# Two bytes instead of four for half words on the wire of a kernel's own clock

## The chip, the cores and the metric

One core of a Trainium2 chip. The metric is the device time of one execution in microseconds, from the first to the last instruction with what lies around them. TensorE is called PE in the profile, VectorE DVE, ScalarE ACT, GpSimd POOL, and SyncE, whose queue issues nearly all transfers, SP.

## The reference

Two blocks work on the same input `x` of 2048 tokens by 576 channels, and a gate mixes them. Cut to what matters:

```
g = sigmoid((x * gate_w).sum(-1))
# A: a long convolution; K is made from 128 complex exponentials per channel (the "taps")
K = einsum("dn,dnl,dn->dl", C, exp(dt * A * l), dt * B).real
a = irfft(rfft(u, 2L) * rfft(K, 2L))[:L] + u * Dskip
# B: product keys: 32 heads, two halves of 64 keys each, top 2 of both halves, 2 of the 4 pairs
q = x @ w_q;  s1 = q1 @ k1.T;  s2 = q2 @ k2.T
top_e, g2 = best two of the four sums and their softmax
act = gelu(x . u[top_e]);  b = sum(g2 * act * v[top_e])
return g * a + (1 - g) * b
```

## The kernel before, in words

The kernel computes dense what the reference gathers. There are two large families of products of half words (fp16, split in a high and a low part), each of 128 groups of 14 matmuls of 128 by 512: the scores `s` (tokens against keys, the query weights folded into the keys by small matmuls `wb`, after which DVE takes the 8 largest and their places) and the activations `a` (tokens against the 4096 rows of `u`), which are scaled into `go` and stored to `g_d` in DRAM.

Beside them run three stages of the convolution:

- The generation of the taps. Pairs of channel groups give matmuls `kb`; ACT and DVE split the result in half words `ko`, and 18 stores write it to `k_d`. In the same stretch a first transform of the input runs (`u`, with tables `tu`; results go to `su_d`).
- The first transform of the taps (`freq`, then `k_stage1`). Four loads, one for each quarter `j`, bring the taps back from `k_d` into the tile `ksb`, and two loads bring the tables `tk0` and `tk16`. Then come 32 steps `k1_0` to `k1_31` of 4 matmuls each, whose results are copied to `k1o` and stored to `sk_d`. All 128 of these matmuls read `ksb`; the first sixteen steps read `tk0`.
- The products in the frequency domain: 36 groups `pr`, `pi`, `pv`, with results stored to `z_d`.

When the scores and activations end, the kernel hands over to the last stage. For each of 16 blocks of 128 tokens, `prep` builds one-hot matrices on DVE (`A`, `Be`, `Bg`), spreads the gates with matmuls `S`, multiplies them into the activations `gl`, and splits the product into half words `wh`. Then 192 matmuls `o` multiply with the rows of `v`, which `v_work` has split into eight chunks `vhl0` to `vhl7`. A chunk costs two copies or scalings for each of four parts on ACT and four differences on DVE (some on POOL). The inverse transform `y` of the convolution is added to each block. The first blocks are 0, 15, 1 and 14.

Nobody writes the order of the instructions by hand. The source runs the whole program once on a clock of its own: every engine call adds a cost (`act_cost`, `dve_cost`, `mm`), every stage is a generator that yields until its inputs are ready by that clock, and the order in which the calls are made is the order in which the instructions stand in each engine's queue. On the chip the engines then wait for one another through semaphores; the source's clock has no part in that. So a cost that is changed moves instructions, and changes no instruction itself.

For transfers the function `dma` (L199) keeps two numbers: `queue`, with 0.45 for each issue, and `wire`, which grows by the bytes of the transfer at 3.4e5 bytes per microsecond. A tile counts as loaded 2.2 after `wire`. Two places read this: every generator that waits for a loaded tile, and the loop in `freq` that paces the loads of the taps:

```
for j in range(4):
    while wire[0] > clock[0] + 2:
        yield 0.3
    dma(ksb[:, j]..., k_d[:, 32 * j:32 * j + 32]...)
```

L133 is the one line through which all ACT, DVE and POOL instructions are recorded, L213 that of all matmuls, and L204 that of all transfers.

Of the kernel before, what the change touches and what calls it, by code (L numbers as in the profile page):

```python
# [13 lines left out]
F16 = mybir.dt.float16  # L14
BF16 = mybir.dt.bfloat16
# [122 lines left out]
def body(ctx: ExitStack, tc: tile.TileContext, xT, au, par, logdt, dskip, gatew, wq, kT, uT, vv,  # L138
# [11 lines left out]
    wire = [0.0]  # L150
# [5 lines left out]
    def key(x):  # L156
        n = x.tensor.name
        return (n, x.offset) if n in columns else n

    def size(x):  # L160
        n = 1
        for d in x.shape[1:]:
            n *= d
        return n
# [34 lines left out]
    def dma(o, i, q=None):  # L199
        t = max(clock[0], rdy.get(key(i), 0.0), queue[0])  # L200
        queue[0] = t + 0.45
        wire[0] = max(wire[0], t) + 4 * o.shape[0] * size(o) / 3.4e5
        rdy[key(o)] = max(rdy.get(key(o), 0.0), wire[0] + 2.2)
        (q or DQ).dma_start(o, i)  # L204

# [95 lines left out]
    def row(x, name, pool):  # L301
        t = pool.tile([128, D], F32, name=name)
        dma(t, bass.AP(tensor=x.tensor, offset=x.offset, ap=[[0, 128], [1, D]]))
        return t
# [7 lines left out]
    def au_load(a, t):  # L312
        for d, o in au_rows(au, t, a):
            dma(o, d)
# [108 lines left out]
    def x_load(tb):  # L423
        a = slot([4, 512], F32, f"xs{tb}")
        r = pl.tile([128, 512], F32, tag="xr", name=f"xr{tb}", bufs=2)
        c = slice(512 * tb, 512 * tb + 512)
        dma(a, xT[0:512, c].rearrange("(k p) n -> p k n", p=128))
        dma(r[0:64], xT[512:576, c])
        dma(r[64:128], xT[512:576, c])
        return a, r  # L430
# [1132 lines left out]
    while groups or acts:  # L1563
# [5 lines left out]
        if groups and bank_free() and lag < (6.0 if not a_ok else 2.0 if not turn_s else 5.0 if kdone[0] < NCK else 8.0):  # L1569
            c, t = groups[0]  # L1570
# [113 lines left out]
```

## Time and profile before

| | |
|---|---|
| median of 3 runs | 1466.44 us (1465.94 to 1466.64) |
| the profiled execution's own time | 1466.58 us |
| its span, first to last instruction | 1464.7 us |
| PE busy | 1431.2 us, 98% of the span |
| DVE busy | 1248.5 us, 85% |
| ACT busy | 790.6 us, 54% |
| POOL busy | 532.0 us, 36% |
| mean granted TensorE clock | 0.995 |
| read from and written to DRAM | 147.51 and 71.30 MB |

Busy shares are of the whole span. Matmuls overlap in the pipeline, so PE can be busy while one matmul waits for nothing but its turn; what counts for the end is where PE stands idle with work left. Times in the views are microseconds from the start of the span. A row of a timeline gives start, duration, engine, line, operation, output tile, input tiles, form and count, and in brackets the idle time before it and what ended that.

### The profile page before, as it was taken

What the parts mean: (1) busy time and instruction counts of PE and PEld (TensorE: products, weight loads), DVE (VectorE), ACT (ScalarE), POOL (GpSimd) and SP (SyncE); (2) the same over time, 40 slices, a digit from 0 to 9 for tenths busy, and PEclk for the clock granted to TensorE, in tenths of its full rate; (3) what the DMA queues carried; (4) which work ended last, traced back from release to release, by engine and by line L of the source; (5) the groups of instructions that cost most, each with busy time, mean ns of one, the idle gap of its engine ahead of it and who ended that gap; (6) DMA issues with size and microseconds to landing.
All of it is one profiled execution on the core that took longest, in us unless ns stands there. A gap on an engine that the chain in (4) does not pass through costs nothing.

```text
span 1464.7 us, 36789 instructions
## 1 busy us (share of the span) xinstructions
PE 1431.2 (98%) x14025; PEld 858.4 (59%) x14028; DVE 1248.5 (85%) x4589; ACT 790.6 (54%) x1315; POOL 532.0 (36%) x511
## 2 busy tenths in 40 slices
PE   5999999999999999999999999998999999999999
PEld 2445454554544544555555444455787787788787
DVE  6989989989999699959899898579998998898860
ACT  5647767698697787434656544576424224223310
POOL 0443545556745645201246799622100110110100
PEclk8999999999999999999999999999999999999999
DMA  9235433372434534384768666677533432442400
GB/s 319 81 93 162 128 94 118 111 213 89 147 104 133 160 107 135 109 263 138 254 211 290 232 200 206 221 239 221 157 111 116 133 125 85 138 147 68 156 10 17
DMA packets 139185, 221.21 MB, mean 151 GB/s; under 512 B 11648, under 2 KB 82688, under 8 KB 132608
## 3 DMA queue, kind: packets, MB, share of 16 engines
q1 hardware_dynamic: 138912, 218.78, 46.5%
q8 instruction: 110, 1.80, 0.5%
q14 instruction: 67, 0.55, 0.1%
q10 hardware_dynamic: 96, 0.07, 0.0%
HBM read 147.51 MB, written 71.30 MB: 149 GB/s over the span
## 4 chain that ended last, share of the span: by engine, by line
PE 84%; DVE 10%; DMA 3%; ACT 1%; issue 1%; SPq 1%; POOL 1%; DVEq 0%; ACTq 0%; POOLq 0%
PE o L213 24%; PE a L213 23%; PE s L213 22%; PE S L213 4%; PE wb L213 2%; PE kb L213 2%; DVE i L133 2%; PE pr L213 2%; DVE m L133 1%; PE u L213 1%; PE y L213 1%; PE kP L213 1%; DVE e L133 1%; PE pv L213 1%; DVE uh L133 1%
## 5 line engine op out<-in xcount | busy, mean ns | idle before, releaser
L213 PE MATMUL o<-vhl,wh 128*128 128x288 f16 x3072 | 387.0, 286 | 0.0
L213 PE MATMUL s<-whl,xb 128*128 128x512 f16 x1536 | 369.5, 382 | 5.0 <-DVE whl L133 4.2
L213 PE MATMUL a<-xb,uhl 128*128 128x512 f16 x1536 | 361.1, 379 | 0.4 <-DVE ko L133 0.4
L213 PEld LDWEIGHTS <-wh 128*128 128x128 f16 x3072 | 296.0, 98 | 76.3 <-issue 3.7
L213 PEld LDWEIGHTS <-xb 128*128 128x128 f16 x1792 | 171.8, 98 | 213.1 <-issue 27.1
L213 PEld LDWEIGHTS <-uhl 128*128 128x128 f16 x1536 | 148.2, 98 | 175.7 <-issue 2.8
L133 DVE FIND_INDEX8 i<-m,s 128x8 uint32<-128x64 f32 x1024 | 206.5, 222 | 0.0
L133 ACT ACTIVATE wh<-gl,s_wg 128x1024 f16<-128x1024 f32 x64 | 68.9, 1137 | 200.3 <-DVE gl L133 200.3
L133 DVE MAX8 m<-s 128x8 f32<-128x64 f32 x1024 | 146.4, 215 | 28.1 <-PE s L213 27.8
L133 POOL TENSOR_TENSOR CS<-CS,ex 128x512 f32<-128x512 f32 x72 | 100.2, 1423 | 139.0 <-DVE ex L133 120.0
L133 POOL TENSOR_TENSOR ya<-ya,db 128x576 f32<-128x576 f32 x16 | 32.0, 2012 | 305.2 <-DMA ya<-in_au_dram 143.6
L133 ACT ACTIVATE go<-a,i_a 128x512 f32<-128x512 f32 x95 | 64.2, 686 | 82.5 <-PE a L213 54.7
L133 POOL TENSOR_TENSOR e<-aN,rt 128x512 f32<-128x512 f32 x72 | 87.5, 1234 | 50.9 <-PE kb L213 47.6
L133 DVE SCALAR_TENSOR_TENSOR wh<-gl,s_wg,wh 128x1024 f16<-128x1024 f32 x64 | 92.4, 1474 | 11.3 <-ACT wh L133 11.3
L133 DVE TENSOR_TENSOR gl<-S,gl 128x256 f32<-128x256 f32 x256 | 90.0, 415 | 7.3 <-PE S L213 7.3
L133 DVE TENSOR_TENSOR Bg<-Be,vals 128x1024 f16<-128x1024 f16 x128 | 90.6, 749 | 2.2
L133 ACT ACTIVATE gl<-gl 128x1024 f32<-128x1024 f32 x64 | 63.5, 1045 | 34.8 <-DMA gl<-g_d 34.8
L133 DVE TENSOR_TENSOR A<-iota_a,vals 128x2048 f16<-128x2048 f16 x64 | 80.5, 1258 | 0.0
L213 PE MATMUL S<-Bg,A 128*128 128x64 f16 x2048 | 73.0, 193 | 5.1 <-DVE Bg L133 4.2
L213 PEld LDWEIGHTS <-A 128*128 128x128 f16 x2048 | 70.6, 97 | 11.2 <-DVE Bg L133 4.1
L213 PE MATMUL s<-wrem,xb 128*128 128x512 f16 x256 | 76.2, 379 | 0.0
L213 PE MATMUL a<-xb,wrem 128*128 128x512 f16 x256 | 76.2, 379 | 0.0
(203 smaller groups left out, 2205.7 us busy)
## 6 DMA issues: line engine op xcount, KB each, us to landing
g_d<-go SPq DMA_DIRECT2D x128, 256.0 KB, 2.7
gl<-g_d SPq DMA_DIRECT2D x32, 1024.0 KB, 5.4
wq<-in_wq_dram SPq DMA_DIRECT2D x16, 1152.0 KB, 6.3
us<-in_au_dram SPq DMA_DIRECT2D x64, 144.0 KB, 3.0
su_d<-us SPq DMA_DIRECT2D x32, 288.0 KB, 2.6
sk_d<-k1o SPq DMA_DIRECT2D x32, 288.0 KB, 2.8
vn<-in_vv_dram SPq DMA_DIRECT2D x32, 288.0 KB, 3.7
ui<-su_d SPq DMA_DIRECT2D x16, 576.0 KB, 4.0
```

Of the source, the lines that this page charges most:

```text
L133: return f(*a, **k)
L213: T.matmul(o, l, r, start=start, stop=stop)
```

## The change

One factor in `dma`. Until now each element of a transfer counted four bytes on the wire; now an element counts two where the destination is fp16 or bf16.

```
     def dma(o, i, q=None):
         t = max(clock[0], rdy.get(key(i), 0.0), queue[0])
         queue[0] = t + 0.45
-        wire[0] = max(wire[0], t) + 4 * o.shape[0] * size(o) / 3.4e5
+        wire[0] = max(wire[0], t) + (2 if o.dtype in (F16, BF16) else 4) * o.shape[0] * size(o) / 3.4e5
         rdy[key(o)] = max(rdy.get(key(o), 0.0), wire[0] + 2.2)
         (q or DQ).dma_start(o, i)
```

By the shapes, four kinds of transfer are counted anew, on the source's clock: a load of `ksb` (128 x 18 x 256 half words) from 6.94 to 3.47, a table `tk` (128 x 4096) from 6.17 to 3.08, a store of `ko` (128 x 1024) from 1.54 to 0.77, and a table `tu` (128 x 256) from 0.39 to 0.19. All other transfers are of 4-byte elements. The number and the forms of the instructions stay; their order changes on every engine from the generation of the taps on, up to about the fifth token block, and is the same again after that.

The first place is SP's queue at the loads of the taps. `go6_1_1` and its like are activations on their way to `g_d`, `wq5_1` is the second half of the query weights of chunk 5. Before:

```order
L204 DMA k_d_68<-ko_7597 128x1024
L204 DMA ksb_7659<-k_d_68 128x18x256
L204 DMA wq4_1_7753<-in_wq_dram 128x2304
L204 DMA g_d_65<-go6_1_0_7783 128x4x128
L204 DMA ksb_7659<-k_d_68 128x18x256
L204 DMA g_d_65<-go6_1_1_7804 128x4x128
L204 DMA g_d_65<-go6_1_2_7823 128x4x128
L204 DMA g_d_65<-go6_1_3_7844 128x4x128
L204 DMA ksb_7659<-k_d_68 128x18x256
L204 DMA wq5_0_7905<-in_wq_dram 128x2304
```

Here follow two more stores to `g_d`, the fourth load of `ksb`, and the two tables. Now:

```order
L204 DMA k_d_68<-ko_7824 128x1024
L204 DMA ksb_7855<-k_d_68 128x18x256
L204 DMA g_d_65<-go6_1_1_7865 128x4x128
L204 DMA ksb_7855<-k_d_68 128x18x256
L204 DMA wq5_1_7982<-in_wq_dram 128x2304
L204 DMA ksb_7855<-k_d_68 128x18x256 x2
L204 DMA tk0_8070<-in_tk_dram 128x4096
L204 DMA tk16_8072<-in_tk_dram 128x4096
```

Eight transfers stood between the first and the fourth load of `ksb`, apart from the loads of `ksb` themselves; now two stand there. On PE, the last matmuls of the generation (`kb34`) and the first step `k1_0` had 17 groups of `s` and `a` and three halves of the fold `wb` between them; now they have 120 matmuls of such groups (eight and a half) and two halves of `wb`. `k1_0` itself stands inside the same group as before, `s4_7`, but with 102 groups of `a` ahead of it instead of 106.

The second place is DVE's queue at the handover, between the one-hot matrices of the second part of block 15 and the first product with its gates (`gl15_0<-S15_0_0`). Before:

```order
L133 TENSOR_TENSOR Bg15_1_13111<-Be15_1_13109,vals_80 128x1024 x2
L133 SCALAR_TENSOR_TENSOR wh0_1_13094<-gl0_0_12547,s_wg_92,wh0_0_13093 128x1024
L133 SCALAR_TENSOR_TENSOR vhl4_12478<-vhl5_12686,sci_76,vhl4_12478 128x576
L133 SCALAR_TENSOR_TENSOR wh0_1_13094<-gl0_0_12547,s_wg_92,wh0_0_13093 128x1024
L133 SCALAR_TENSOR_TENSOR wh0_1_13094<-gl0_1_12548,s_wg_92,wh0_0_13093 128x1024
L133 SCALAR_TENSOR_TENSOR vhl5_12686<-vhl6_12687,sci_76,vhl5_12686 128x576
L133 TENSOR_SCALAR go7_2_0_13218<-a7_2_0_13149,i_a_91 128x512
L133 TENSOR_TENSOR gl15_0_13096<-S15_0_0_13179,gl15_0_13096 128x32x8
```

Now:

```order
L133 TENSOR_TENSOR Bg15_1_13173<-Be15_1_13171,vals_80 128x1024 x2
L133 SCALAR_TENSOR_TENSOR wh0_1_13102<-gl0_1_12722,s_wg_92,wh0_0_13101 128x1024
L133 SCALAR_TENSOR_TENSOR vhl7_12691<-vs_12937,sci_76,vhl7_12691 128x576
L133 SCALAR_TENSOR_TENSOR wh0_1_13102<-gl0_1_12722,s_wg_92,wh0_0_13101 128x1024
L133 TENSOR_SCALAR go7_2_2_13284<-a7_2_2_13218,i_a_91 128x512
L133 TENSOR_TENSOR gl15_0_13158<-S15_0_0_13250,gl15_0_13158 128x32x8
```

At this point the splitting of `v` stood at chunks 4 and 5 and now stands at the last, 7. From the last gates of block 0 (`S0_3`) on, DVE had seven differences of `vhl` still ahead of it and now has three; the other four stand ahead of `S0_3`, after the last scores.

More of the change, by code (lines that the diff above doesn't have):

```diff
@@ L201, in dma @@
         queue[0] = t + 0.45
-        wire[0] = max(wire[0], t) + 4 * o.shape[0] * size(o) / 3.4e5
+        wire[0] = max(wire[0], t) + (2 if o.dtype in (F16, BF16) else 4) * o.shape[0] * size(o) / 3.4e5
         rdy[key(o)] = max(rdy.get(key(o), 0.0), wire[0] + 2.2)
```

## The prediction

> **What bounds the kernel now.** I read the page first: the span, the busy shares, the slices and the chain of work that ended last.
>
> ```profile
> span 1464.7 us, 36789 instructions
> PE 1431.2 (98%) x14025; PEld 858.4 (59%) x14028; DVE 1248.5 (85%) x4589; ACT 790.6 (54%) x1315; POOL 532.0 (36%) x511
> ...
> PE   5999999999999999999999999998999999999999
> DVE  6989989989999699959899898579998998898860
> ...
> PEclk8999999999999999999999999999999999999999
> ...
> PE 84%; DVE 10%; DMA 3%; ACT 1%; issue 1%; SPq 1%; POOL 1%; DVEq 0%; ACTq 0%; POOLq 0%
> ```
>
> PE is busy 1431.2 of 1464.7 us, so all that an order can win or lose at once is the 33.5 us in which PE stands idle, and whatever new idle time it makes. The change removes no instruction and alters none, so the sum is a sum of waits. The next view is therefore the list of what PE waited for (total, times, longest, in us).
>
> ```profile
> PE x L213 <- ACT xb L133: 4.5, 1, 4.5
> PE S L213 <- DVE Bg L133: 4.2, 6, 2.3
> PE s L213 <- DVE whl L133: 4.2, 1, 4.2
> PE sq L213 <- ACT uhl L133: 4.0, 1, 4.0
> PE kn L213 <- ACT vals L133: 3.1, 1, 3.1
> PE pi L213 <- DVE m L133: 1.7, 1, 1.7
> PE k L213 <- ACT k1o L133: 1.4, 1, 1.4
> PE y L213 <- DMA tf<-in_tf_dram: 1.0, 1, 1.0
> PE kb L213 <- issue: 1.0, 1, 1.0
> ...
> PE S L213 <- DVE ya L133: 0.7, 1, 0.7
> ...
> PE k L213 <- DVE i L133: 0.6, 1, 0.6
> ```
>
> The waits for `xb`, `whl`, `uhl` and `vals` (15.8 us together) belong to the start, where the order is the same in both kernels; they stay. What is open to the change is short: the two waits of the taps' transform (`k`, 2.0 us), the one of the products (`pi`, 1.7), and the handover (`S` and `y`, up to 5.9). None of them is a wait for the taps' loads: at the place that the change is about, PE does not wait today.
>
> **The loads of the taps, the price.** Now the change, first where it acts: the four loads of `ksb`. Their time and PE's work around them before:
>
> ```profile
> 606.43 0.29 PE L213 MATMUL kb<-e,CS 128*32 128x64 f32 x8
> ...
> 638.68 2.75 PE L213 MATMUL s<-whl,xb 128*128 128x512 f16 x12
> ...
> 641.70 2.75 PE L213 MATMUL s<-whl,xb 128*128 128x512 f16 x12
> ...
> 652.20 2.32 PE L213 MATMUL wb<-kt,wq 128*64 128x64 f32 x72
> 654.45 1.47 PE L213 MATMUL s<-whl,xb 128*128 128x512 f16 x6
> 662.88 0.65 PE L213 MATMUL k<-ksb,tk 128*128 128x288 f16 x4
> ```
>
> From the last `kb` (606.43) to `k1_0` (662.88) lie 56.5 us, and `k1_0` shows no wait: 56.5 us of cover were enough for loads that went out over 28 us. The new order leaves 120 matmuls of groups `s` and `a` and two halves of `wb`. A group of 14 takes 3.02 us (638.68 to 641.70), so 120 take 120/14 x 3.02 = 25.9; a half of `wb` takes 2.25 (652.20 to 654.45), two 4.5; with the 0.29 of `kb` itself, **PE reaches `k1_0` 30.7 us after the start of the last `kb`.**
>
> What must have landed by then is `ksb` whole and `tk0`. The rows for it (in the windows: start and end, length, then busy PE, PEld, DVE, ACT, POOL, the granted clock, the DMA share and GB/s):
>
> ```profile
> 612.57 0.77 SPq L204 DMA_DIRECT2D ksb<-k_d  x1
> ...
> 640.16 0.68 SPq L204 DMA_DIRECT2D ksb<-k_d  x1
> ```
>
> ```profile
> DMA to landing us min/median/max: 6.7/6.8/6.9
> ```
>
> ```profile
> 614.60:617.60 3.00, 3.00 (x65) 2.11 (x64) 3.00 (x25) 0.52 (x1) 0.00 (x0) 1.00 0.95 274
> 619.40:621.40 2.00, 2.00 (x11) 0.90 (x10) 1.99 (x7) 0.70 (x3) 0.00 (x0) 1.00 1.03 438
> 648.40:651.40 3.00, 3.00 (x15) 1.36 (x14) 2.72 (x26) 0.00 (x0) 0.00 (x0) 1.00 1.02 428
> ```
>
> The first window holds a `ksb` load alone: 274 GB/s at a DMA share of 0.95, so the engines are full, and the short pieces of this gather, not the queue, set its pace. By its shape a load is 1.18 MB, at 274 GB/s 4.3 us; of the landing's 6.8 that leaves 2.5 of latency. The second window holds a load of `wq` (1.18 MB, at 438 GB/s 2.7 us), the third a table `tk` (1.05 MB, at 428 GB/s 2.45 us). In the new queue stand the four loads, one `g_d` store (0.26 MB, 1.0 us at the slow rate), `wq5_1` and `tk0`. The first load goes out 612.57 - 606.43 = 6.1 us after `kb`, since its stores to `k_d` come first, and I keep that. Then 6.1 + 2.5 + 4 x 4.3 + 1.0 + 2.7 + 2.45 = **32.0 us**, which is 1.3 behind PE. `wq5_1` has to wait on SP for PE to finish with the half that it overwrites, but two loads of `ksb` are ahead of it to keep the engines full meanwhile.
>
> So a new wait of **+1.3** at `k1_0`, between 0 and 8.9: if the loads ran one behind the other with their whole landing of 6.8 us, 6.1 + 4 x 6.8 + 1.0 + 2.7 + 2.45 = 39.5, 8.8 to 8.9 behind PE. I stay near the lower end, because several loads in flight share a latency and the share of 0.95 says that the rate is the limit. Nothing on PE can pass `k1_0`, so the wait counts in full; behind it on PE stands the rest of group `s4_7`, so DVE's search of the 8 largest comes later by as much.
>
> **What a wait costs beyond itself.** The clock of PE is the second price.
>
> ```profile
> 707.86 0.70 PE L213 MATMUL k<-ksb,tk 128*128 128x288 f16 x4 [1.41 <-ACT k1o L133]
> 888.88 0.43 PE L213 MATMUL pi<-ui,cst 64*64 64x256 f32 x2 [1.67 <-DVE m L133]
> 1007.61 0.20 PE L213 MATMUL S<-Bg,A 128*128 128x64 f16 x1 [2.26 <-DVE Bg L133]
> ```
>
> ```profile
> 890.40:893.90 3.50, 3.50 (x9) 1.09 (x9) 2.59 (x11) 1.23 (x4) 3.42 (x4) 0.51 0.97 311
> ```
>
> After the wait of 1.67 us at 888.88 the granted clock was 0.51 for 3.5 us (890.4 to 893.9), a loss of about 1.75 us; after the 1.41 and the 2.26 it was not. One in three, so a new wait of this size is charged 1.75/3 = **+0.6**. The Trainium skill (TensorE: Matmul & The Clock Gate, Part 1) puts the step down of the clock after at least one idle window of about 3.4 us. The trace does not agree: 1.67 us was enough once. By the page this term would be 0 and the time 0.6 us less.
>
> **The waits of the taps' transform and the products.** The three waits of these stages (1.4, 0.6, 1.7) and the low clock (1.75) make 5.5 us. They hang on which engine's queue holds what, and the new order shuffles these stages: the products end some 22 us earlier in PE's work, with 26 rather than 22 groups of `a` left behind them. How tight it is there:
>
> ```profile
> 750.00:890.00 140.00, 138.33 (x1345) 67.90 (x1343) 130.40 (x841) 75.54 (x200) 110.94 (x123) 1.00 0.65 223
> ```
>
> DVE is busy 130.40 of 140 us, so PE can be caught up again at other places. Bounds: -5.5 if all go, +5.5 if as much again comes. I take **-1.2**: two thirds of one low clock's 1.75, since such a loss followed one wait in three and the order has to hit that place anew; the waits themselves I take as moved and not gone. The generation of the taps, whose waits are of 1.0 us and less, I take at **0**, between -2 and +2 (twice the largest of its rows).
>
> **The handover.** The busy time there, before it and in it:
>
> ```profile
> 925.00:983.70 58.70, 58.70 (x511) 29.56 (x509) 36.09 (x77) 37.20 (x74) 23.48 (x28) 1.00 0.72 231
> 983.70:1039.70 56.00, 50.51 (x512) 33.78 (x509) 55.72 (x75) 33.52 (x42) 16.77 (x11) 1.00 0.69 216
> ```
>
> ```profile
> L133 DVE SCALAR_TENSOR_TENSOR vhl<-vhl,sci,vhl 128x576 f16<-128x576 f32 x5 | 4.0, 808 | 0.0
> L133 DVE SCALAR_TENSOR_TENSOR vhl<-vs,sci,vhl 128x576 f16<-128x576 f32 x2 | 1.6, 803 | 0.0
> ```
>
> From 983.7 to 1039.7 DVE works 55.72 of 56 us and PE stands idle 5.5 (56.00 - 50.51): this is the one stretch where DVE is the bound, and what ends the waits is DVE's `Bg` and `ya`. Just before, DVE has room (36.09 of 58.70). In the stretch stand the seven differences of `vhl` (5 + 2 rows) that the order shows behind `S0_3`. Now three stand there, and four are moved to where DVE has room: 4 x 0.808 = **-3.2**. Bounds: -5.5, all of PE's idle time there; +1, a late table like the `y <- tf` row, which is late next once DVE is not. The stores and loads that SP issues are the same ones, and no row of PE's waits names a `go` buffer, so the `g_d` stores now queued behind the tables cost nothing; their cover is the ring of `go` buffers, and if it ran out a group `a` would wait about one table's 2.45 us.
>
> **The sum.** -3.2 + 1.3 + 0.6 - 1.2 + 0 = **-2.5 us**. The profiled execution took 1466.58 us (span 1464.7, 1.9 around it), so 1464.1; it stands 0.14 above the median of 1466.44, so **1463.9**. What a measurement of this kernel can tell from no change is about 0.2%, 2.9 us.
>
> **The rivals.**
>
> *A, the other side: the loads run into one another.* The price is the wait of 8.9 with a low clock behind it (1.75): 8.9 + 1.75 - 3.2 - 1.2 = +6.3, **1472.7**. It decides once `tk0` lands more than some 4 us behind PE's arrival (4 + 0.6 - 3.2 - 1.2 = 0.2, and with the low clock certain 1.4). For it: the cover falls from 56.5 to 30.7 us, and landings of 6.8 us were measured with the loads apart, never together. Against it: the share of 0.95. Chance 0.21.
>
> *B, no wait at all.* If neighbouring loads stream at the 428 of the tables, 1.18 MB is 2.8 us, and the sum of the loads is 6.1 + 2.5 + 4 x 2.8 + 6.2 = 26.0, 4.7 ahead of PE: the terms 1.3 and 0.6 go, -4.4, **1462.0**. Against it: 274 GB/s in the row with the engines full. Chance 0.17. The Trainium skill (DMA: Bandwidth & Descriptors, the section on the anatomy of one DMA) fits a transfer as 2.0 us and its bytes at 436 GB/s, which is 4.7 us for such a load and this case; the rows show 6.8.
>
> *C, the gain is given back.* DVE is full through the handover, and what leaves it may be replaced by products of later blocks, so that PE waits as before; the transform's waits likewise. Then -2.5 becomes about 0, between -1 and +4 with a new wait or two in the products: **1466.4**. For it: 130.40 of 140. Chance 0.14.
>
> *D, all goes well.* The waits of the transform and products go with the low clock (-5.5) and the handover gains 3.2, no wait at `k1_0`: -8.7, **1457.7**. Chance 0.12.
>
> **How the numbers follow.** The forecast has 0.36, with a range of its own of 1460.5 to 1467 (the handover between -5.5 and +1 around the other terms). The spread over faster, same and slower by 2.9 us is: forecast 0.18, 0.15, 0.03; A 0, 0, 0.21; B 0.14, 0.03, 0; C 0, 0.06, 0.08; D 0.12, 0, 0. Together 0.44, 0.24, 0.32. The range reaches from just under D to A's value, 1457.5 to 1473.0; left out are the far tails of A, C and D.
>
> **What would show it.** Right: the row of `k1_0` has a wait of 0 to 3 us named by `tk` or `ksb`; between the last scores and block 1's `gl` PE's idle time is about 2 us rather than 5.5, with three `vhl` differences behind `S0_3`; the `k`, `pi` waits sum to some 3.7 us. Wrong: `k1_0` waits 5 us or more (A); the landing of `ksb` stays at 6.8 with all four in flight (B); PE's wait for `Bg` is 3.8 us as now (C); or PE waits in the generation of the taps or in the products for something that isn't in the list above, by more than 3 us.

## The result, and the profile after

| | before | after |
|---|---|---|
| median of 22 runs each | 1467.68 us (1465.18 to 1469.06) | 1467.24 us (1463.89 to 1470.91) |
| ratio | | 1.0002, 95% interval 0.9994 to 1.0009 |
| profiled execution's span | 1464.7 us | 1464.3 us |

The three runs ahead of the prediction are among the 22 of the kernel before. The change makes no difference that these runs can tell: the interval is -0.9 to +1.3 us. The gain of 2.5 us that was forecast lies outside it, though the median lies in the stated range, which reached from 1457.5 to 1473.0. The order was turned over on all five engines, and the time stood still; so the question is which parts gained, and where that went.

PE's busy time by stage in the one profiled execution of each kernel, first before, then after (start and end, length, busy time of PE, PEld, DVE, ACT, POOL, granted clock, DMA share, GB/s):

```profile
0.00:300.00 300.00, 282.24 (x2351) 141.05 (x2355) 266.31 (x1085) 196.94 (x303) 132.27 (x107) 0.98 0.45 141
300.00:612.00 312.00, 309.64 (x3092) 156.74 (x3090) 279.57 (x1006) 241.48 (x348) 173.01 (x136) 1.00 0.42 127
612.00:750.00 138.00, 136.04 (x1061) 73.16 (x1060) 110.33 (x793) 67.60 (x179) 19.54 (x64) 1.00 0.68 227
750.00:940.00 190.00, 188.33 (x1782) 90.46 (x1780) 163.72 (x1027) 99.80 (x267) 155.87 (x175) 0.99 0.63 216
940.00:1110.00 170.00, 164.34 (x1765) 113.33 (x1764) 155.25 (x246) 90.34 (x124) 30.22 (x20) 1.00 0.59 188
```

```profile
0.00:300.00 300.00, 282.73 (x2351) 142.32 (x2355) 266.05 (x1085) 194.78 (x300) 132.04 (x107) 0.99 0.45 141
300.00:612.00 312.00, 308.48 (x3024) 156.18 (x3022) 280.43 (x1053) 239.32 (x347) 167.20 (x132) 0.99 0.41 127
612.00:750.00 138.00, 134.56 (x1207) 72.42 (x1206) 112.92 (x760) 73.76 (x192) 38.44 (x78) 1.00 0.69 233
750.00:940.00 190.00, 187.74 (x1738) 90.77 (x1736) 161.89 (x1014) 101.41 (x277) 149.97 (x176) 1.00 0.66 223
940.00:1110.00 170.00, 168.30 (x1757) 115.05 (x1754) 150.31 (x236) 82.62 (x110) 26.24 (x17) 1.00 0.55 177
```

Length less PE's time is PE's idle time. The handover (940 to 1110) gains 4.0 us: 5.66 idle before, 1.70 after. The generation of the taps loses 1.2 (2.36 to 3.52), the taps' transform 1.5 (1.96 to 3.44), the products 0.6 (1.67 to 2.26).

One trace of each kernel is little for differences of this size. Four of the experiments below (`before_pool`, `before_nopool`, `skip_pool`, `skip_dve`) have the order of before up to 940, and one (`after_hold`) has that of the changed kernel, so they repeat these three stages. PE is idle there for 6.0, 5.5, 4.8, 5.2 and 4.5 us in the five traces of the old order, and for 9.2 and 9.5 in the two of the new. The generation (1.7 to 2.4 against 3.5 and 4.2) and the transform (1.3 to 2.5 against 3.4 and 4.3) are worse in every one of these traces; the products (1.0 to 1.7 against 2.3 and 1.1) can't be told apart.

The waits after, beside those of the start:

```profile
PE pr L213 <- DMA ki<-sk_d: 2.7, 2, 1.5
...
PE wn L213 <- ACT wj L133: 2.2, 2, 1.1
PE S L213 <- DVE Bg L133: 2.0, 4, 0.8
PE a L213 <- DVE i L133: 2.0, 1, 2.0
PE pi L213 <- DVE m L133: 1.0, 1, 1.0
...
PE k L213 <- issue: 0.6, 1, 0.6
```

Gone are `k` for `k1o` (1.4), `y` for `tf` (1.0) and half of the waits for `Bg`; of `pi`'s 1.7 there is 1.0 left. New are `ki`, `wj` (one of its two waits is in the generation, one in the transform), and `a` for `i`. The half clock (a stretch in which the granted clock is 0.5) moved too: behind the products' wait before, now behind the new wait in the generation. In `after_hold` the same wait for `i` has none behind it, and the one half clock stands at 710.7 instead.

```profile
415.34 2.19 PE L213 MATMUL a<-xb,uhl 128*128 128x512 f16 x6 [2.01 <-DVE i L133]
```

```profile
415.90:419.30 3.40, 3.40 (x11) 1.37 (x9) 3.23 (x10) 1.43 (x3) 3.40 (x4) 0.51 0.00 0
```

And the loads of the taps, on SP and PE:

```profile
630.71 0.78 SPq L204 DMA_DIRECT2D ksb<-k_d  x1
...
646.65 4.45 SPq L204 DMA_DIRECT2D tk<-in_tk_dram  x2
```

```profile
625.44 0.29 PE L213 MATMUL kb<-e,CS 128*32 128x64 f32 x8
...
657.18 0.65 PE L213 MATMUL k<-ksb,tk 128*128 128x288 f16 x4 [0.63 <-issue]
```

`k1_0` starts 31.7 us after the last `kb` (the prediction had 32.0 for the loads), and PE was there 31.1 us after it (30.7), so 0.63 us of wait. The profile names no cause for it ("issue"), but the landings of the two tables `tk` show one:

```profile
DMA to landing us min/median/max: 8.9/9.7/10.4
```

The longer of the two is that of `tk0`, which went out at 646.65 and landed 10.4 us later, at 657.1, just ahead of `k1_0`.

### The profile page after: what moved, and what is told of

It reads as the page before. It is cut to its first block, busy times and chain, and to the rows that moved or that the text cites. A ratio compares the mean times of both kernels' runs of the same rounds, so it can differ in the third digit from the quotient of the medians.

```text
span 1464.3 us, 36807 instructions
## 1 busy us (share of the span) xinstructions
PE 1431.7 (98%) x14025; PEld 859.7 (59%) x14028; DVE 1242.3 (85%) x4578; ACT 786.4 (54%) x1318; POOL 535.0 (37%) x517
## 4 chain that ended last, share of the span: by engine, by line
PE 85%; DVE 7%; DMA 3%; POOL 2%; ACT 1%; issue 1%; SPq 0%; DVEq 0%; ACTq 0%; POOLq 0%
PE o L213 24%; PE a L213 23%; PE s L213 22%; PE S L213 4%; PE wb L213 2%; PE kb L213 2%; PE pr L213 2%; DMA sk_d<-k1o 1%; PE y L213 1%; DMA ki<-sk_d 1%; PE u L213 1%; PE kP L213 1%; DVE wh L133 1%; PE pv L213 1%; DVE e L133 1%
## 5 line engine op out<-in xcount | busy, mean ns | idle before, releaser
L213 PEld LDWEIGHTS <-xb 128*128 128x128 f16 x1792 | 171.3, 98 | 212.7 <-issue 25.9
L133 ACT ACTIVATE go<-a,i_a 128x512 f32<-128x512 f32 x90 | 60.9, 686 | 92.2 <-PE a L213 63.8
L133 DVE TENSOR_TENSOR Bg<-Be,vals 128x1024 f16<-128x1024 f16 x128 | 83.8, 696 | 2.2
L133 DVE MATCH_VALUE_LOAD i<-m,s 128x8 f32 x1024 | 75.8, 74 | 0.2
```

Of the source, the lines that this page charges most:

```text
L133: return f(*a, **k)
L213: T.matmul(o, l, r, start=start, stop=stop)
```

## The experiments

Every part of the change acts through the order, so each can be made alone: the factor is two for one kind of transfer and four for the others. This was done for `tu` and for `ksb`, not for the tables `tk` or the stores of `ko` alone. The theories: **1**, the time is a sum of waits, and the handover's wait is due to the differences of `vhl` on DVE behind `S0_3`; **2**, DVE is full there anyway and whatever it is spared is taken up by other work; **3**, formed after the second set, POOL's differences hold DVE's operations. The idle time of the handover is 170 us less PE's busy time from 940 to 1110.

### The parts of the change

The edit in `dma`, here for `only_tu`; `only_ksb` has size 4608, `not_tu` has `!= 256`, and `one_byte` has 1 in place of 2 without the condition on the size:

```diff
-(2 if o.dtype in (F16, BF16) else 4)
+(2 if o.dtype in (F16, BF16) and size(o) == 256 else 4)
```

**only_tu**

> Two bytes only for the tables tu (0.39 to 0.19 on the source's clock, the smallest of the four kinds), all else four. By the order this alone brings the changed kernel's order of the generation of the taps, from matmul 3003 on; at the handover ten differences of vhl then stand behind S0_3 (seven before, three in the changed kernel), and k1_0 has 48 us of PE work behind the last kb. Theory 1, the sum of waits: PE's idle time in the handover goes with the number of these differences, 5.5 us at seven and 1.05 at three, so 1.1 each and about 8.8 at ten; the new wait of a for i (2.0 us) near 413 appears as in the changed kernel; no wait at k1_0. Some 4.5 us slower than before, about 1472. Theory 2, the gain is given back wherever DVE is full: the number doesn't decide, PE's idle time in the handover stays between 4 and 6, time within 1.5 us of before.

Measured: 1473.26 us beside 1466.34, ratio 1.0050 (1.0038 to 1.0062). Theory 1 was near in the time (about 1472). The wait of `a` for `i` is there, 2.0 us, as in the changed kernel; the handover is idle 7.3 us, all of it for `Bg`:

```profile
PE S L213 <- DVE Bg L133: 7.3, 7, 2.9
```

Three half clocks (867.7, 973.5 and 1041.8) against one before add some 3.4 us. The smallest of the four counts, 0.2 of the source's clock, so costs more alone than the largest, that of `ksb`, which comes next.

**only_ksb**

> Two bytes only for the loads of ksb, all else four. The generation of the taps has the order of before; 36 us of PE work between the last kb and k1_0 (56 before, 31 in the changed kernel); five differences of vhl behind S0_3. Theory 1: idle in the handover 5.5 - 2 x 1.1 = 3.3 us; no wait of a for i near 413; the loads, ready some 32 us after kb, are no wait; 2.2 us faster than before, about 1465.5. Theory 2: handover idle 4 to 6 us, time within 1.5 us of before.

Measured: 1469.69 us, ratio 1.0029 (1.0017 to 1.0041): slower, where both theories had faster or the same. The handover did gain (3.8 us idle, 5.7 before), but new waits of PE for `wj` came, 5.0 us in four, among them 3.3 us near 720, where ACT had the scaling of `wj` behind copies of `k1o` that waited themselves (5.4 us put down to PE's `s`, 1.0 to stores to `sk_d`). The other 1.7 lie near 134, where the order is that of before, so they are no effect of the edit. No row of before had shown a wait at `wj`.

**not_tu**

> The change without its part for the tables tu (ksb, tk, ko at two bytes, tu at four). Generation of the taps as before, 33 us of PE work between the last kb and k1_0, four differences of vhl behind S0_3, and 20.5 us of PE work between the last step of k1 and the first products (13 in the changed kernel). Theory 1: handover idle about 2.2 us, no wait for i near 413, at k1_0 0 to 0.5, the first wait for ki gone since the store to sk_d has 7 us more: 3 to 4 us faster than before, about 1464. Theory 2: within 1.5 us of before.

Measured: 1462.99 us, ratio 0.9981 (0.9969 to 0.9992). Faster, as theory 1 had it: no wait for `i`, none for `ki`, and 1.5 us idle in the handover. One new wait stands at the taps' transform, followed by a half clock (651.1 to 654.5):

```profile
650.99 1.05 PE L213 MATMUL k<-ksb,tk 128*128 128x288 f16 x4 [2.75 <-ACT k1o L133]
```

**one_byte**

> One byte for every element of a half-word destination, so half of the changed kernel's count again. The four loads of ksb stand together in SP's queue with the tables behind them, and only 18.7 us of PE work lie between the last kb and k1_0; four differences of vhl behind S0_3. Theory 1, the loads at the price of the prediction: 5.3 + 2.5 + 4 x 4.3 + 2.45 = 27.5 us after kb until tk0 is there, so a wait of 8.7 us at k1_0, with a half clock behind it (1.75) in some runs; handover idle 2.2 instead of 5.5; 1472 to 1475. Rival B of the prediction, loads that stream at 428 GB/s: 21.5 us, a wait of 2.8 us, about 1467. If each load took its whole landing of 6.8 us, 35 us and a wait of 16, about 1481.

Measured: 1487.44 us, ratio 1.0147 (1.0133 to 1.0162). The wait at `k1_0`, with the loads that end it:

```profile
616.31 12.54 SPq L204 DMA_DIRECT2D ksb<-k_d  x4
628.90 4.45 SPq L204 DMA_DIRECT2D tk<-in_tk_dram  x2
```

```profile
639.66 2.08 PE L213 MATMUL k<-ksb,tk 128*128 128x288 f16 x8 [8.94 <-DMA tk<-in_tk_dram]
```

8.94 us where the prediction's price gives 8.7, streaming at 428 GB/s 2.8, and landings one behind the other 16. With four loads in flight the engines moved 295 GB/s from 619.5 to 625.5, near the 274 of one load, and the four loads landed 4.0 to 4.1 us after one another, the table 2.5 after the last. The rest of the loss is a wait of `u` for `uh` of 5.1 us near 311 and one for `tt` of 3.6 near 847, with half clocks of 6.8, 6.8 and 3.4 us beside the three (`k1_0`, `uh`, `tt`).

### The handover

**after_hold**

```diff
             h = vt[c]
+            while c >= 6 and not spread:
+                yield 0.5
             yield from ready(raw[c])
```

`spread` is filled when `S0_3` is issued.

> The changed kernel, but v_work holds the chunks 6 and 7 back until S0_3 has been issued. The order of everything up to the handover stays; behind S0_3 stand six differences of vhl instead of three. Theory 1, the differences on DVE are the cause: PE's idle time from 940 to 1110, 1.7 us in the changed kernel and 5.7 before, rises to about 4.3, named by Bg, and the kernel takes 2 to 3 us more than the changed one, 1469 to 1470. Theory 2, the place of the differences is a by-product and the idle time comes from what else the order holds there (the earlier end of the products): idle stays at 1.7 us, the time at 1467.

Measured: 1466.43 us beside 1466.99, ratio 0.9998 (0.9985 to 1.0011). Theory 1 falls here: with six differences behind `S0_3` the handover is idle 0.7 us, less than with three.

**before_pool**

```diff
-                    if G.free < clock[0] + 1 and S.free < V.free:
+                    if c >= 4 or G.free < clock[0] + 1 and S.free < V.free:
```

> The kernel before with its order up to the last chunks of v; from chunk 4 on all differences of vhl go to POOL, with the scaling on ACT that the kernel has for this path. No difference of vhl is left on DVE behind S0_3 (seven before), POOL has 16.8 of 56 us and ACT 33.5 of 56 to do there. Theory 1: idle 940 to 1110 falls from 5.7 us to 1 or less, and the kernel is 4 to 5 us faster than before, about 1462, without any change to the clock of the source. Theory 2: PE waits as before, for Bg or for something else, and the time stays within 1.5 us of before. Between the two lies a wait of the products o for the late chunk 7 on POOL (1.3 to 1.7 us each there, eight of them), which would name vhl.

Measured: 1471.76 us, ratio 1.0028 (1.0016 to 1.0040). With no difference on DVE at all the handover is idle 7.8 us, more than before (5.2 for `Bg`, 2.2 for `ya`, 0.4 at `y`).

**not_tu_tk** and **not_tu_tk_pool**

```diff
-        tabs = load(0), load(16)
+        tabs = [load(0)]
...
+            if w == 6:
+                tabs.append(load(16))
             tkt = tabs[w // 16]
```

> The change without its part for tu, and the second table tk16 loaded at step 6 of k1 instead of ahead of step 0. In the kernel without this edit PE waited 2.75 us at 647.95 for k1o, behind the stores to sk_d whose landing took up to 9.5 us, and the clock was halved behind it. Theory 1, the two tables and wq keep the first stores to sk_d back: the wait falls below 1 us, 2 to 4 us faster than that kernel (1463 beside 1466.3 for before), so 4 to 7 faster than before. Otherwise the wait stays, at another step, and the time is that of the kernel without this edit, 3 faster than before.

Measured: 1462.03 us beside 1466.99, ratio 0.9961 (0.9947 to 0.9974). The wait for `k1o` is gone from PE's list and no half clock is left between 60 and 1455 us. This beats the kernel before, and the changed one by its ratio (1.0002); those two were not run in one set.

> Both edits together on the change without its part for tu: tk16 at step 6, and the differences of vhl on POOL from chunk 4 on (none on DVE behind S0_3 instead of four). Theory 1: idle 940 to 1110 falls from 1.5 us to 0.5, 1 us faster than without the pool edit, 5 to 8 faster than before. Theory 2: no gain from the pool edit, or a loss where ACT's 8 extra scalings or POOL come late.

Measured: 1469.18 us, ratio 1.0013 (0.9999 to 1.0028): the pool edit costs 7 us and not the gain of 1; PE waits 6.0 us for `Bg` in the handover, and not at all for it without the pool edit.

Both pool kernels speak against theory 1, and the traces say why. DVE and POOL in the kernel before, with POOL's differences of `vhl` and DVE's `Bg` side by side:

```profile
1015.54 1.28 POOL L133 TENSOR_TENSOR vhl<-vhl,vhl 128x576 f16<-128x576 f32 x1 [10.63 <-ACT vhl L133]
1019.60 1.28 POOL L133 TENSOR_TENSOR vhl<-vs,vhl 128x576 f16<-128x576 f32 x1 [2.79 <-DMA yz<-z_d]
```

```profile
1015.64 2.32 DVE L133 TENSOR_TENSOR Bg<-Be,vals 128x1024 f16<-128x1024 f16 x2
...
1019.74 3.51 DVE L133 TENSOR_TENSOR Bg<-Be,vals 128x1024 f16<-128x1024 f16 x2
```

Two `Bg` take 1.29 us where POOL rests; here 2.32, and 3.51 where POOL goes on with `ya`. In the groups of DVE from 983.7 to 1039.7 the mean of a `Bg` is 992 ns before, and in the changed kernel, in `after_hold` and in `before_pool`, in this order:

```profile
L133 DVE TENSOR_TENSOR Bg<-Be,vals 128x1024 f16<-128x1024 f16 x14 | 9.1, 689 | 0.2
```

```profile
L133 DVE TENSOR_TENSOR Bg<-Be,vals 128x1024 f16<-128x1024 f16 x14 | 9.1, 688 | 0.2
```

```profile
L133 DVE TENSOR_TENSOR Bg<-Be,vals 128x1024 f16<-128x1024 f16 x14 | 15.2, 1126 | 0.2
```

That goes with POOL's number of differences in the same stretch: seven before, three after, two in `after_hold`, fourteen in `before_pool`. But the number alone does not decide it; it matters what stands beside them on DVE. Before, four of the seven ran beside a `Bg` or a `wh` (2.31 us instead of 1.27). After, none of the three did: one ran beside products `gl`, two beside the building of an `A`, which took 2.30 instead of 1.21:

```profile
991.05 1.71 POOL L133 TENSOR_TENSOR vhl<-vs,vhl 128x576 f16<-128x576 f32 x1 [5.07 <-ACT vs L133]
```

```profile
991.54 2.30 DVE L133 TENSOR_TENSOR A<-iota_a,vals 128x2048 f16<-128x2048 f16 x1
```

The last set was to tell theory 3 from theory 1 with the queues left as they were.

**skip_pool** and **skip_dve**

```diff
                         S.activation(x, x, AF.Copy, scale=sv[0])
                         yield from ready(raw[c])
+                        G.mute = c >= 4
                         G.tensor_sub(h[:, j, 1, :], x, h[:, j, 0, :])
+                        G.mute = False
+                        if c >= 4:
+                            nc.scalar.activation(h[:, j, 1, :], x, AF.Copy)
```

A muted call is counted on the source's clock and not issued, so the order of what is left stays, apart from the copies added on ACT. The edit leaves out the two POOL differences of each of the chunks 4 to 7, so eight, not the eleven that the expectation below counts. `skip_dve` does the same to the differences on DVE, eight too.

> The kernel before, with POOL's differences of vhl left out from chunk 4 on (11 instructions, ten of them between 960 and 1036); ACT writes a copy in their place, so the low half of these rows of v is wrong. DVE's queue is the same, instruction for instruction, with its seven differences behind S0_3. Theory 3, formed on the last runs: an operation of DVE on half words that runs beside one of POOL's differences is held until that ends (Bg 1.7 to 1.9 us instead of 0.69), and this, not the number of DVE's own differences, makes the handover slow. Then DVE's Bg fall to 0.69, PE's idle time from 940 to 1110 falls from 5.7 us to about 1, and the kernel is 4 to 5 us faster, about 1462. Theory 1, DVE's own differences are the cause: idle stays near 5.7, time within 1 us of before.

Measured: 1467.76 us beside 1466.55, ratio 1.0017 (1.0005 to 1.0029). Half of theory 3 came true: the mean `Bg` falls to 756 ns and the waits for `Bg` and `ya` from 4.5 to 1.1 us, with DVE's queue unchanged. But nothing of it reached the end (the interval even lies a little above 1), since PE now waits at the first inverse transform:

```profile
1022.96 3.42 PE L213 MATMUL y<-yz,tf 128*32 128x288 f32 x32 [5.37 <-DMA gl<-g_d]
```

(The profile names `gl`, but `y` reads `yz` and `tf`, and `tf` was issued just ahead of `gl`.)

> The kernel before, with DVE's differences of vhl left out from chunk 4 on, the seven behind S0_3 among them; ACT writes a copy in their place, so the low half of these rows of v is wrong. POOL's queue is the same. Theory 1: DVE has 5.6 us less in the stretch, idle falls from 5.7 us to 1 or less, 4 to 5 us faster. Theory 3: the stretched Bg stay (1.7 us and more), idle falls by 2 to 3 us at most, since a held Bg makes PE wait at its own place; 2 to 3 us faster.

Measured: 1465.14 us, ratio 0.9996 (0.9984 to 1.0007), no difference that can be told. 3.9 us idle, 3.5 of them for `Bg`, whose mean is 1066 ns, and one of these waits (3.1 us) comes with a half clock of 6.8 us. Theory 3 had the waits; the gain of 2 to 3 us did not come.

**before_nopool** and **not_tu_tk_nopool**

```diff
-                    if G.free < clock[0] + 1 and S.free < V.free:
+                    if c < 4 and G.free < clock[0] + 1 and S.free < V.free:
```

> The kernel before, all differences of vhl on DVE from chunk 4 on, none on POOL: twelve behind S0_3 instead of seven. Theory 1, 0.9 us of idle time for each: 10 us idle from 940 to 1110, some 4 us slower than before. Theory 3: 5 x 0.8 us of work more on DVE and 9.5 us of its stretch in the handover gone, idle 2 to 5 us, time between 3 us faster and the same.

Measured: 1473.24 us, ratio 1.0056 (1.0038 to 1.0074). Slower than either theory, and theory 1's 10 us of idle time (8.6 measured) come for another reason: only 2.7 us are for `Bg`, and 5.9 are at `y`. ACT shows how:

```profile
1007.74 1.50 ACT L133 ACTIVATE vhl<-vhl,sci 128x576 f16<-128x576 f32 x2 [4.96 <-DVE vhl L133]
1009.15 0.67 ACT L133 ACTIVATE go<-a,i_a 128x512 f32<-128x512 f32 x1
```

The last `go` stands on ACT behind a scaling that waits for a difference on DVE, and the loads for `y` stand behind the store of that `go`. Nor was this kernel the plain test of theory 3 that it was meant to be: the source's order now gives POOL two `wh` instead (2.81 and 2.24 us), beside which a `Be` took 2.62 us and a `Bg` 2.49, where either takes 0.69 alone. So with no difference on POOL the mean `Bg` is still 919 ns.

> The fastest kernel so far (the change without its part for tu, tk16 at step 6; 5 us faster than before) with all differences of vhl on DVE from chunk 4 on. Its idle time from 940 to 1110 was 1.2 us, a wait for the table tf, so there is little left. Theory 3: the same time within 1.5 us, and Bg without its long cases. Theory 1: six differences behind S0_3 instead of four, 2 us slower.

Measured: 1463.61 us beside 1466.55, ratio 0.9977 (0.9965 to 0.9988). In the handover the waits for `Bg` are 0.4 us (none without the edit), and that at `y` is 2.2 (1.2 without it). By its ratio it lies behind the kernel without the edit (0.9961), but the intervals overlap, so this run decides between none of the theories.

## Why the prediction was right or wrong

**The loads of the taps: right, to 0.7 us.** The loads came 31.7 us after the last `kb` (32.0), the wait was 0.63 (1.3), and at twice the pressure the price held again (8.94 against 8.7). The parts hold too: the last two loads of `ksb` and `tk0` landed at 650.3, 654.6 and 657.1, so 4.3 and 2.5 us apart, as priced. A little luck is in the total: the first load went out 5.3 us after `kb` rather than 6.1, and the rest took 26.4 rather than 25.9. Rivals A and B fall: the loads neither run one behind the other nor stream like a table. (The fit of the Trainium skill that the prediction sets beside rival B is stated there for transfers issued from GpSimd; these loads go out on SP's queue, and the forecast did not use it.)

**The half clock: one chance for two kinds of wait.** In the 14 traces, from 60 us on, a half clock came beside 13 of 21 waits of PE of 1.5 to 2.5 us and 8 of 9 longer ones, but only 2 of 27 of 1.0 to 1.5. So one in three was too much for the wait of 1.3 that the prediction expected, and the wait of 0.63 that came cost only itself. Any new wait over 1.5 us should have been charged some 1.2 (an estimate: 21 of 30, 1.7 us each). The changed kernel has as many half clocks as before, one.

**The generation of the taps: the step that failed first.** It stood at 0 between -2 and +2. It lost 1.2 us of idle time, and with the half clock that moved there (some 1.7 more) it lies outside those bounds. The term was judged by the size of the waits in the trace of before, but a new order makes waits at places where that trace shows none. That `tu`'s part brings the wait for `i` is shown: `only_tu` has the same one, `not_tu` has none.

**The taps' transform and the products: too hopeful.** -1.2 was forecast, for the half clock alone, with the waits moved and not gone. The half clock did leave the products (1.7 us), and the waits for `k1o` and `m` did go or shrink. But `ki` and `wj` took their place, so that the waits of the two stages grew by 2.1 us (1.5 and 0.6), of which 0.63 is the one at `k1_0` that the prediction had put elsewhere. This is rival C at another place than it was put. The same order up to the handover gave in `after_hold` no wait for `ki` but 2.7 us for `wj`, so how these share it is not fixed by the order alone.

**The three stages together.** Ahead of the handover the prediction added up to +0.7 (1.3 + 0.6 - 1.2 + 0). The idle time there grew by 3.2 us, with one half clock in both kernels. The difference, 2.5 us, is as large as the gain that did not come. One of the prediction's own signs of being wrong says the same: PE waited 4.4 us in the generation and the products for things that stood in no row of its list (`a` for `i` 2.0, `wj` 1.1, `ki` 1.2).

**The handover: the sum about right, the reason wrong.** -3.2 was forecast and -4.0 measured, inside the bounds. But the step was "four differences on DVE x 0.808". `after_hold` put three of them back and lost nothing; `skip_dve` took away all and left 3.9 us idle. Missing was POOL's half of the same chunks. In the new order seven differences of POOL in the stretch became three, and none of these met a `Bg`: the `Bg` fell from 13.3 to 9.1 us, 3.1 of it from three differences that had each held one and the rest from a `ya` of POOL that had. `skip_pool` shows that this is a cause of the waits for `Bg` and `ya`, since it took away POOL's differences and left DVE's queue as it was (with copies on ACT in their place).

Missing also was the second chain, put down as "+1, a late table". The loads for `y` can't go out before the last stores of `go` have landed, since they use that memory. Before, on PE, ACT, SP:

```profile
1004.75 0.59 PE L213 MATMUL a<-xb,wrem 128*128 128x512 f16 x2
...
1022.09 2.15 PE L213 MATMUL y<-yz,tf 128*32 128x288 f32 x32 [1.03 <-DMA tf<-in_tf_dram]
```

```profile
1005.38 0.69 ACT L133 ACTIVATE go<-a,i_a 128x512 f32<-128x512 f32 x1 [2.17 <-PE a L213]
```

```profile
1001.70 0.47 SPq L204 DMA_DIRECT2D vs<-in_vv_dram  x1
1006.10 0.36 SPq L204 DMA_DIRECT2D g_d<-go  x1
1009.93 0.34 SPq L204 DMA_DIRECT2D db<-in_dskip_dram  x1
...
1016.60 0.59 SPq L204 DMA_DIRECT2D tf<-in_tf_dram  x1
```

From the last `a` to `y` are 17.3 us, and in this trace no link of that chain is work of DVE: the last `go` on ACT, its store, the loads behind it (`db` goes out when the store has landed), `y`. In that time PE waits 3.7 us (2.26, 0.39 and 1.03) in the kernel before. After:

```profile
1006.68 0.59 PE L213 MATMUL a<-xb,wrem 128*128 128x512 f16 x2
```

```profile
1022.48 2.15 PE L213 MATMUL y<-yz,tf 128*32 128x288 f32 x32
```

```profile
1008.08 0.36 SPq L204 DMA_DIRECT2D g_d<-go  x1
1010.48 0.35 SPq L204 DMA_DIRECT2D db<-in_dskip_dram  x1
```

15.8 us without a wait, so PE has 15.80 - (17.34 - 3.68) = 2.1 us more work between the two. And the chain itself is 1.5 us shorter, nearly all of it at the last store: from its issue to `db` are 3.8 us before and 2.4 after. Before, the load `vs` of the last chunk of `v` stands just ahead of it (it landed at 1007.74); after, that load went out at 964. In `skip_pool`, where `vs` is in the way again, these are 5.2 us, and from the last `a` to `y` 20.1:

```profile
1004.24 0.36 SPq L204 DMA_DIRECT2D g_d<-go  x1
1009.44 0.35 SPq L204 DMA_DIRECT2D db<-in_dskip_dram  x1
```

That `vs` is what holds the store is read from these rows; no run moves it alone. The changed order eases both chains, by luck, since nothing in the change aims at either. That easing the first alone is worth nothing is shown by `skip_pool`; the second alone was not tried, and what each gave of the 4.0 us can't be split.

**The sum.** Idle time of the two profiled executions: start -0.5, generation +1.2, transform +1.5, products +0.6, handover -4.0, together -1.2 us up to 1110. PE's busy time is 0.5 us longer and the tail behind its last matmul 0.3, so the spans differ by 0.4. A gain of 4 us was paid back in the stages ahead of it, 3.2 us in this pair of traces.

## What to carry to other kernels

When a change only turns the order over, price the stretch that is bound by an engine, and charge the rest of the program something for new waits: here about 3 us net, in waits that no row of the trace before showed. At a place where several chains meet, find the second one before counting what the first is worth; the time that a step takes away from it can be lost whole, as in `skip_pool`. A model of transfers in a source is worth correcting per stage: the same correction gained 3 us without `tu` and cost 7 us with `tu` alone. Whether it gains where it does because the model is truer, or because another order happens to be better, these runs don't tell: the orders that do the whole work have ratios from 0.9961 to 1.0147.

## What the runs showed of the hardware

An operation of DVE with two inputs in SBUF that runs beside a POOL operation is held: `Bg` took 0.69 us alone and up to 1.89 beside POOL in the kernel before, `wh` 1.27 and up to 2.43, `A` 1.21 and 2.34. Moving eight differences of 0.8 us from DVE to POOL went with a loss of 5 us in `before_pool`. `gl`, which has one input in PSUM, took 0.41 beside POOL as alone. The Trainium skill (SBUF — State Buffer, "Who interferes with whom") states that a DVE operation with two inputs in SBUF and a POOL operation that reads SBUF shut one another out for the whole instruction. The trace agrees, by `Bg` (two inputs in SBUF, 1.89) and `gl` (one, 0.41); the prediction did not weigh it.

A wait of PE of 1.5 us can bring 3.4 us at half clock, and one of 5 to 9 us brought 6.8 more than once. The Trainium skill (TensorE: Matmul & The Clock Gate, Part 1) puts the step down behind at least one idle window of about 3.4 us; 13 of 21 shorter waits here speak against that.
